# Scores of four heads on four 32-row strips, from keys and queries transposed as channel pairs

## The chip, the cores and the metric

One core of a Trainium2 chip runs the whole program. The metric is device time in microseconds of one execution. The core has TensorE (PE; its weight loads are listed as PEld), VectorE (DVE), ScalarE (ACT), GpSimd (POOL) and SyncE (SP), each with its own queue in which instructions run in order, and 16 DMA engines that serve the DMA queues. TensorE reads from SBUF and writes to PSUM, which has eight banks of 2 KB per partition.

## The reference

Attention with two fixed masks, then a bilinear feed-forward layer. For 8 batches, 8 heads, 576 positions and 64 channels:

```python
scores = scale * np.matmul(q, k.transpose(0, 1, 3, 2))
mask_local = (rel >= 0) & (rel < stride)                       # heads 0 to 3, stride 32
mask_strided = (rel >= 0) & (pos[None, :] % stride == pos[:, None] % stride)   # heads 4 to 7
attn = softmax(np.where(mask, scores, -1e9))
x = (attn @ v) laid out as 4608 tokens x 512
out = ((x @ w_a) * (x @ w_b)) @ w_out                          # w_a, w_b: 512x1536, w_out: 1536x512
```

## The kernel before

**Two interleaved streams.** The feed-forward layer runs over nine tiles of 512 tokens. Each tile has 16 slots, and slots are numbered through (tile t starts at slot 16t). The first twelve slots of a tile form one 128-wide slice f of the hidden layer each: `ab_mm` (L617) multiplies by `w_a` and `w_b` (L626), ScalarE copies the first product out of PSUM (`a_sb`, L647) and VectorE multiplies it by the second into `pf` (L650). The last four slots form the output y of the tile. In tiles 0 and 1 these are plain matmuls (L892); from tile 2 on `y_plan` (L815) forms y from fourteen groups of six products (L830, the order in `Y_ORDER`), which need `pf` and sums of it that VectorE makes in `fast_s` (L754). PSUM tiles `mm` (three banks) and `tp` (one) are shared in turn by all of these; `st` and `o` have two banks each and serve the attention.

**Attention rides on the slots.** Batch b must be ready when tile b needs its tokens, so its steps are written by hand into the slots of tile b-1: table `STEPS` for batches 1 and 2, `LATER` and `IN_Y` (L584 to L592) for batches 3 to 7. A position n means after slot n; n - 0.5 means in the middle of slot n, between the products with `w_a` and `w_b`; a position in `IN_Y` counts the groups of y. What a step issues on every engine takes its place in that engine's queue there.

A batch has eight units u: two pairs of local heads (u = 0 to 3) and two of strided heads (u = 4 to 7), each in two halves. A unit takes two steps:
- `S` (L437): `S_p` multiplies keys by queries into `st` (L392), `S_x` takes the exponential on ScalarE into `p` (L413), `S_m` masks `p` on VectorE (L431).
- `V`: `V_p` multiplies `p` by the values into `o` (L470), and VectorE divides by the sums (L478, L496). For strided units from batch 2 on, and for all units of batch 2, `step_VT` (L518) is used instead: L529 forms the transposed output in `o`, ScalarE takes Ln of the sums and Exp of its negative (L538, L539), and VectorE multiplies into `xT` (L543, L545). Local units of batches 3 to 7 go to DRAM and come back transposed (`rows_out`, `rows_in`: steps O and I).

**Keys and queries from batch 2 on.** GpSimd issues loads that cast to bf16, each of the four heads of a kind on its own 32 partitions. `step_D` (L320) transposes them on VectorE in blocks of 32x32, as 2-byte elements: two calls each for local k and q (L329), three each for strided k and q (L334). After that the two halves of a head's 64 channels lie side by side, so 24 SyncE copies per batch (L346, L350) bring them to 64 partitions, the queries into `qz`, in which the other head's half stays zero. `kT` and `qz` are double-buffered. Then one matmul of 128 rows gives both heads of a pair:

```python
nc.tensor.matmul(sv[:, i, :2 * n].rearrange("p (j n) -> p j n", j=2), lhsT=kT[:, c % 2, k0:k0 + 128],
                 rhs=qz_pair[b % 2][c // 2][:, :, c % 2, k0:k0 + n], start=True, stop=True)
```

The zeros are set by memsets early on (`zero_qz`, L114) and again for batch 3 by GpSimd (`rezero`, L355). The calls `do(slot, ...)` (L1021 to L1059) place loads, transposes and memsets; where a slot has any, GpSimd first runs a one-element copy (`pace`, L1076) that waits for the slot's result. Batch 0 scores its heads one by one, each on 64 of the 128 rows (L405, for strided heads after a first product L399).

Of the kernel before, what the change touches and what calls it, by code (L numbers as in the profile page):

```python
# [9 lines left out]
I16 = mybir.dt.int16  # L10
ALU = mybir.AluOpType
# [3 lines left out]
FIRST_D = 2  # L15
# [16 lines left out]
def kernel(  # L32
# [34 lines left out]
    def open_psum(stack, **bufs):  # L67
        for nm, n in bufs.items():
# [8 lines left out]
    qz_pair = [(const.tile([128, 2, 2, S], BF16, name=f"qz{i}l"), const.tile([128, 2, 2, RS * GP], BF16, name=f"qz{i}s"))  # L77
               for i in range(2)]
    qz_buf = [[tuple(t[:, j] for t in pair) for j in range(2)] for pair in qz_pair]
    kT_buf = [(const.tile([128, 2, PAD + S], BF16, name=f"kT{i}l"), const.tile([128, 2, RS * GP + 48], BF16, name=f"kT{i}s"))  # L80
              for i in range(2)]
    vl_buf = [const.tile([128, HL * 6, VW], BF16, name=f"vl{i}") for i in range(2)]
# [15 lines left out]
    def consts(i):  # L98
        if i == 0:
            for p in p_buf:  # L100
                nc.vector.memset(p[:, :, W:], 0.0)
            nc.vector.memset(p_buf[4][:, 1, 2 * W - PW:W], 0.0)
        nc.vector.memset(kT_buf[i][0][:, :, 0:PAD], 0.0)
        nc.vector.memset(kT_buf[i][1], 0.0)
        nc.vector.memset(vl_buf[i][:, :, D:D + 1], 1.0)
        nc.vector.memset(vs_buf[i][:, :, :, D:D + 1], 1.0)
        nc.vector.memset(vl_buf[i][:PAD, 0, 0:D], 0.0)
# [4 lines left out]
    spare = qz_buf[0][0][0][:, 0]  # L112

    def zero_qz(i, eng, parts=((0, 0), (0, 1), (1, 0), (1, 1))):  # L114
        for j, z in parts:
            t = qz_buf[i][j][z]
            if (i, j, z) == (0, 0, 0):
                t = t[:, 1]
            if eng is nc.scalar:
                nc.scalar.copy(t, spare[:, :1].unsqueeze(2).to_broadcast(list(t.shape)))  # L120
            else:
                eng.memset(t, 0.0)
# [176 lines left out]
    def T_e(b, c, nm):  # L299
        tv = held.pop((b, c, nm))  # L300
        if c < 2:
            perm = lambda t: t.rearrange("d (p r) -> d p r", r=RL)
        else:
            perm = lambda t: t.rearrange("d (g p) -> d g p", p=GP)[:, :, :NP]
        if nm == "k":
            t = kT_buf[b % 2][c // 2][:, c % 2]
            (nc.scalar.copy if b == 1 and c < 2 else nc.vector.tensor_copy)(perm(t[:, PAD:] if c < 2 else t[:, :RS * GP]), tv)
        elif b == 0:
            if c % 2 == 0:
                tl[b, c // 2, nm] = blocks("q", c // 2)  # L310
            nc.scalar.copy(perm(tl[b, c // 2, nm][:, c % 2]), tv)
        else:
            for j in range(2):
                pr = slice(64 * j, 64 * j + 64)
                nc.scalar.copy(
                    perm(qz_buf[b % 2][j][c // 2][pr, c % 2]), tv[pr])
# [3 lines left out]
    def step_D(b, z, nm, part):  # L320
        src = nats.get((b, nm, z == 1))
        if part == 0:
            tl[b, z, nm] = blocks(nm, z)
        t = tl.get((b, z, nm))
        if part is None:
            last = True
        elif z == 0:
            i = slice(NY // 2 * part, NY // 2 * (part + 1))
            nc.vector.transpose(t.rearrange("p h (i y) -> p i h y", i=NY)[:, i],  # L329
                                src[:, i].rearrange("p i (h d) -> p i h d", h=2))  # L330
            last = part == 1
        else:

            nc.vector.transpose(  # L334
                t.rearrange("p h (r c) -> p r h c", r=RS)[:, :, :, YS * part:YS * part + 32],
                src[:, part].rearrange("p (r h d) -> p r h d", r=RS, h=2))
            last = part == 2
        if last:
            for nm, c in {"k": (("k", 0),), "q": (("q", 0), ("k", 1), ("q", 1)), "r": (("k", 1), ("q", 1))}[nm]:
                if part is not None and z == 1 and c == 1 and b > FIRST_D:  # L340
                    continue
                t = tl[b, z, nm]
                for e in range(2):
                    if nm == "k":
                        dst = kT_buf[b % 2][z][64 * e:64 * e + 64, c]
                        nc.sync.dma_start(out=dst[:, PAD:] if z == 0 else dst[:, :RS * GP], in_=t[64 * c:64 * c + 64, e])  # L346
                        continue
                    for j in range(2):
                        r0 = 64 * c + 32 * j
                        nc.sync.dma_start(out=qz_buf[b % 2][j][z][64 * e + 32 * j:64 * e + 32 * j + 32, c],  # L350
                                          in_=t[r0:r0 + 32, e])
                if (nm, c, z) == ("q", 0, 0) and b - 1 > FIRST_D:
                    rows_in(b - 1, 1)

    def rezero(b):  # L355

        for j in range(2):
            for t in qz_buf[b % 2][j]:
                nc.gpsimd.memset(t[32:64] if j == 0 else t[64:96], 0.0)
# [19 lines left out]
    def p_cols(b, p, j, i, n, w):  # L379
        return p[:, j, i * n:i * n + w] if b == 0 else p_flat(p)[:, (2 * i + j) * n:(2 * i + j) * n + w]  # L380

    def S_p(b, u):
# [5 lines left out]
        if b > 0:  # L388
            sv = st.rearrange("p a (i n) -> p (a i) n", n=256)
            for i in range(G):  # L390
                k0 = (G * half + i) * (LW if c < 2 else GP)
                nc.tensor.matmul(sv[:, i, :2 * n].rearrange("p (j n) -> p j n", j=2), lhsT=kT[:, c % 2, k0:k0 + 128],  # L392
                                 rhs=qz_pair[b % 2][c // 2][:, :, c % 2, k0:k0 + n], start=True, stop=True)
            return
# [13 lines left out]
    def S_x(b, u):  # L408
# [3 lines left out]
        if b > 0:  # L412
            nc.scalar.activation(p_flat(p)[:M, :2 * W].rearrange("p (i n) -> p i n", n=2 * n),  # L413
                                 st[:M].rearrange("p a (i n) -> p (a i) n", n=256)[:, :G, :2 * n], ACT.Exp, scale=scale)
            return
        nc.scalar.activation(p[:M, :, :W], st[:M, :, :W], ACT.Exp, scale=scale)

    def S_m(b, u):
        c, half, M, n, G = unit(u)
        p = ps[b, u]  # L420
        at_j = 1 if b == 0 else 2
        shape = [M, 2, G, n] if b == 0 else [M, G, 2, n]
# [4 lines left out]
        if b == 0:  # L427
# [14 lines left out]

    def V_p(b, u):
# [11 lines left out]
        else:  # L455
            o = psum4["o"].tile([128, 2, 512], F32, tag="o", name="o")
# [61 lines left out]
    def step_VT(b, u):  # L518
# [3 lines left out]
        o = psum4["o"].tile([128, 2, 512], F32, tag="o", name="o")  # L522
# [45 lines left out]
    def step_X(b, c):  # L568
# [16 lines left out]
                 10: "V6 Tk0", 10.5: "Tq0 Pk1 Z0", 11: "Pq1", 12: "V7 Tk1 S0 W0 W1", 12.5: "Tq1 W2",  # L585
                 12.6: "S1", 12.75: "L0 X2", 13: "s2 X3 V0 m2 L1 W3", 13.5: "V1 S3", 14: "V2 X0", 14.5: "V3 D1", 15: "X1"},
             2: {20: "S0", 20.5: "S1", 21.5: "V0", 22: "S2", 23: "V1", 23.5: "S3", 24.5: "V2", 25: "S4", 26: "V3", 26.5: "S5",
                 27.5: "V4", 28: "S6", 28.5: "V5", 29: "S7", 29.5: "V6", 30.5: "V7"}}
    LATER = {-1: "S0", 0: "S1", 1: "V0", 2: "S2", 3: "V1 O0", 4: "S3 I0", 5: "V2", 6: "S4", 7: "V3 O1", 8: "S5", 9: "V4",
             10: "S6",  # L590
             11: "V5"}
    IN_Y = {2: "S7", 6: "V6", 11: "V7"}  # L592
    FN = {"Tk": step_Tk, "Tq": step_Tq, "S": step_S, "V": step_V, "X": step_X, "W": lambda b, n: fast_w(n, slice(0, 3)),
          "s": S_px, "m": S_m, "L": lead_vl, "O": rows_out, "I": rows_in, "Pk": lambda b, c: pair_up("k", c), "Pq": lambda b, c: pair_up("q", c),
          "Z": lambda b, n: zero_qz(0, nc.vector, ((1, 1),)), "D": lambda b, n: step_D(FIRST_D, 0, "k", n)}
# [33 lines left out]
    def ffn_ab(t, f, mid, ab=None):  # L629
# [21 lines left out]
        else:  # L651
# [6 lines left out]
              + [t.rearrange("p a b c -> p (a b c)")[:, :12 * 128] for t in qz_pair[0]]]  # L658
    xsum = {t: qz_pair[1][t - 7].rearrange("p a b c -> p (a b c)")[:, :8 * HT].rearrange("p (n c m) -> p n c m", n=4, c=2)
# [261 lines left out]
    with tc.manual_schedule(engines={ENG.PE, ENG.SP, ENG.Pool, ENG.DVE, ENG.Activation}):  # L921
# [20 lines left out]
        zero_qz(1, nc.scalar, ((0, 1),))  # L942
# [9 lines left out]
        for nm in ORDER:  # L952
# [24 lines left out]
            elif nm == "Z":  # L977
                zero_qz(1, nc.scalar, ((0, 0),))
# [25 lines left out]
        steps[16 * (B - 2) + 9][-1][1].append("I1")  # L1004
# [16 lines left out]
        for b in range(FIRST_D, B):  # L1021
            g0 = 16 * (b - 2)
            if b == FIRST_D:
                do(0, load_qk, b, False)
                do(1, load_qk, b, True)
                do(16, load_vl, b)
                for h in range(HL):
                    do(20 + h, load_vs, b, (h,))
            else:
# [5 lines left out]
            gs = {2: (14, 14, 15, 15, 16, 16, 17, 17, 18, 18), 3: (8, 9, 10, 11, 12, 13, 14, 15, 16, 17)}.get(b) or (  # L1035
                3, 5, 7, 9, 12, 13, 14, 15, 16, 17)
            for (z, nm, part), g in zip(((0, "k", 0), (0, "k", 1), (0, "q", 0), (0, "q", 1), (1, "k", 0), (1, "k", 1),
                                         (1, "k", 2), (1, "q", 0), (1, "q", 1), (1, "q", 2)), gs):
                if (b, z, nm, part) != (FIRST_D, 0, "k", 1):
                    do(g0 + g, step_D, b, z, nm, part)  # L1040
            if b > FIRST_D:
                do(g0 + 19, step_D, b, 1, "r", None)
# [9 lines left out]
        do(1, zero_qz, 1, nc.vector, ((1, 1),))  # L1052
        do(4, zero_qz, 1, nc.vector, ((1, 0),))
        for i, jz in ((2, (0, 0)), (3, (1, 0)), (0, (0, 1))):
            do(i, zero_qz, 0, nc.vector, (jz,))
        do(14, rezero, 1)
# [53 lines left out]
```

## Time and profile before

| | |
|---|---|
| time, median of 3 runs | 326.2 us (325.67 to 326.99) |
| span of the profiled execution, first to last instruction | 324.3 us |
| runs' median less that span | 1.9 us |
| granted TensorE clock | 0.999 |
| busy: DVE, ACT, POOL | 259.9, 190.9, 162.7 us |
| moved by DMA | 40.44 MB; mean 125 GB/s |
| L413, exp of a unit | 56 times, 650 ns |
| L431, mask of a unit | 32 times 454 ns, 28 times 448 ns |
| L329 and L334, transposes | 24 times 766 ns; 36 times about 703 ns |

The profile comes from one execution, whose own time is known as its span; the runs beside it were not profiled. A line of a timeline gives start, length, engine, line of the code, operation, what is written and read, shapes, and how many instructions were merged into it. A TensorE row's length is the time from start to result, 190 to 380 ns for one matmul, while the next one starts long before that: how fast matmuls follow each other is seen only from their starts. Some records of matmuls are missing.

### The profile page before, as it was taken

The numbers are of one execution on the slowest core, as the hardware profiler recorded it, in microseconds if no ns is written. First come the engines' busy times: TensorE is split into PE (matmuls) and PEld (weight loads), VectorE is DVE, ScalarE is ACT, GpSimd is POOL, SyncE is SP. The second block draws the span as 40 slices with busy tenths as digits, with TensorE's granted clock in tenths as the row PEclk, the third lists the DMA queues.
The fourth block names the chain that finished last, engine by engine and source line by source line (L and its number), as shares of the span: only waits on it lengthen the run. The fifth ranks groups of instructions, "written<-read, shape, count | busy, mean of one in ns | idle before, by whom it ended". The sixth has DMA issues, their size and how long they took to land.

```text
span 324.3 us, 7477 instructions
## 1 busy us (share of the span) xinstructions
PE 316.7 (98%) x2669; PEld 211.2 (65%) x2698; DVE 259.9 (80%) x563; ACT 190.9 (59%) x338; POOL 162.7 (50%) x293
## 2 busy tenths in 40 slices
PE   8999999999999999999999999999999999999994
PEld 7764555455555577556999895559555866786684
DVE  6766797888878988898889888988999667857862
ACT  6762776468674576447654765467546655535541
POOL 8844938689948534762576338734004003202520
PEclk9999999999999999999999999999999999999999
DMA  8999999899999999999899999999137030004004
GB/s 154 138 203 195 203 191 173 169 173 143 133 224 124 147 88 99 107 187 179 94 111 183 183 108 92 158 205 131 30 81 166 20 115 18 0 2 129 1 3 129
DMA packets 110725, 40.44 MB, mean 125 GB/s; under 512 B 88672, under 2 KB 107744, under 8 KB 110688
## 3 DMA queue, kind: packets, MB, share of 16 engines
q0 software_dynamic: 85968, 19.48, 66.0%
q1 hardware_dynamic: 24576, 20.42, 24.9%
q8 instruction: 21, 0.34, 0.4%
q14 instruction: 16, 0.13, 0.1%
q10 hardware_dynamic: 144, 0.07, 0.1%
HBM read 39.51 MB, written 10.91 MB: 155 GB/s over the span
## 4 chain that ended last, share of the span: by engine, by line
PE 88%; DMA 5%; POOL 4%; DVE 1%; issue 1%; ACT 1%; POOLq 0%
PE mm L626 42%; PE mm L830 17%; PE mm L892 6%; PE mm L710 5%; DMA wb_sb<-in_moe_w_b_dram 5%; PE st L392 4%; PE ax L703 3%; PE mm L703 2%; PE o L529 2%; PE o L470 2%; PE mm L857 2%; POOL shared L197 1%; PE end L857 1%; POOL wa_sb L252 1%; POOL vl L225 1%
## 5 line engine op out<-in xcount | busy, mean ns | idle before, releaser
L626 PE MATMUL mm<-xT,wb_sb 128*128 128x512 bf16 (+1 forms) x381 | 88.2, 352 | 0.7 <-DMA wb_sb<-in_moe_w_b_dram 0.4
L626 PE MATMUL mm<-xT,wa_sb 128*128 128x512 bf16 (+1 forms) x367 | 86.6, 351 | 0.8
L647 ACT COPY a_sb<-mm 128x512 f32<-128x512 f32 x84 | 49.2, 586 | 47.6 <-PE mm L626 45.6
L626 PEld LDWEIGHTS <-wb_sb 128*128 128x128 bf16 x392 | 37.8, 98 | 34.3 <-DMA wb_sb<-in_moe_w_b_dram 1.1
L1076 POOL CAST pace<-pf 1x1 f32<-1x1 bf16 x82 | 24.5, 298 | 64.3 <-DVE pf L650 42.7
L626 PEld LDWEIGHTS <-wa_sb 128*128 128x128 bf16 x392 | 35.1, 98 | 21.1
L650 DVE TENSOR_TENSOR pf<-a_sb,mm 128x512 bf16<-128x512 f32 x62 | 42.1, 679 | 7.3 <-PE mm L626 6.1
L413 ACT ACTIVATE p<-st 72x576 bf16<-72x576 f32 (+1 forms) x56 | 36.4, 650 | 14.4 <-PE st L392 14.2
L545 DVE TENSOR_TENSOR xT<-o,xr 64x288 bf16<-64x288 f32 x48 | 21.4, 446 | 14.8 <-ACT xr L539 14.5
L830 PEld LDWEIGHTS <-ps 128*128 128x128 bf16 x288 | 28.0, 98 | 3.1
L795 ACT COPY y_sb<-mm 128x512 f32<-128x512 f32 (+1 forms) x28 | 15.6, 556 | 17.6 <-PE mm L830 15.0
L830 PE MATMUL mm<-wf,ps 128*128 128x256 bf16 x216 | 25.5, 273 | 0.0
L710 PE MATMUL mm<-xT,wb_sb 128*128 128x512 bf16 x83 | 25.3, 379 | 0.1
L538 ACT ACTIVATE xr<-o 64x576 f32<-64x576 f32 x28 | 18.1, 648 | 12.1 <-PE o L529 11.9
L892 PE MATMUL mm<-wo_sb,pf 128*128 128x512 bf16 x93 | 23.1, 379 | 0.2
L243 POOL DMA_DIRECT2D vs<-in_v_dram x24 | 19.7, 820 | 4.8 <-PE mm L830 2.4
L830 PEld LDWEIGHTS <-pf 128*128 128x128 bf16 x216 | 20.3, 98 | 2.5 <-issue 0.2
L1076 POOL COPY pace<-y_sb 1x1 f32<-1x1 f32 x23 | 4.6, 200 | 33.1 <-DVE y_sb L793 20.1
L539 ACT ACTIVATE xr<-xr 64x576 f32<-64x576 f32 x28 | 19.1, 683 | 0.9
L652 DVE TENSOR_TENSOR pf<-a_sb,mm 128x512 bf16<-128x512 f32 x22 | 14.9, 677 | 4.8 <-ACT a_sb L647 2.7
L212 POOL DMA_DIRECT2D kl<-in_k_dram x24 | 16.0, 667 | 5.2 <-issue 2.9
L830 PE MATMUL mm<-wo_sb,pf 128*128 128x256 bf16 x144 | 18.5, 273 | 0.1
(189 smaller groups left out, 598.0 us busy)
## 6 DMA issues: line engine op xcount, KB each, us to landing
out_dram<-y_sb SPq DMA_DIRECT2D x12, 512.0 KB, 4.8
out_dram<-y_sb SPq DMA_DIRECT2D x11, 256.0 KB, 3.9
vl<-in_v_dram POOLq DMA_DIRECT2D x6, 384.0 KB, 7.8
kl<-in_k_dram POOLq DMA_DIRECT2D x24, 72.0 KB, 3.1
ql<-in_q_dram POOLq DMA_DIRECT2D x24, 72.0 KB, 3.2
vs<-in_v_dram POOLq DMA_DIRECT2D x24, 72.0 KB, 4.3
wo_sb<-in_moe_w_out_dram POOLq DMA_DIRECT2D x4, 384.0 KB, 9.5
natk<-in_k_dram POOLq DMA_DIRECT2D x20, 72.0 KB, 3.6
```

The source lines that it names most:

```text
L243: nc.gpsimd.dma_start(out=vs_buf[b % 2][:, h, :, 0:D], in_=v[b, HL + h].rearrange("(p r) d -> p r d", r=RS))
L413: nc.scalar.activation(p_flat(p)[:M, :2 * W].rearrange("p (i n) -> p i n", n=2 * n), st[:M].rearrange("p a (i n) -> p (a i) n", n=256)[:, ...
L538: nc.scalar.activation(r, sums, ACT.Ln)
L539: nc.scalar.activation(r, r, ACT.Exp, scale=-1.0)
L545: nc.vector.tensor_mul(dst.rearrange("d (p r) -> d p r", r=RS)[:, :, G * half:G * (half + 1)], o[:64, j, :W].rearrange("d (g p) -> d p g", ...
L626: nc.tensor.matmul(ps_[:, c0:c0 + n], lhsT=w[:, kk, 128 * f:128 * (f + 1)], rhs=xT[:, kk, x0:x0 + n], start=(kk == first and c0 == 0), sto ...
L647: nc.scalar.copy(a_sb, ab[0])
L650: nc.vector.tensor_mul(pf[:, f, :].rearrange("p (i a s) -> p a i s", i=2, s=16), halves(a_sb), halves(ab[1]))
L710: nc.tensor.matmul(got[e], lhsT=wb_sb[:, kk, 128 * f:128 * (f + 1)], rhs=xT[:, kk, x0:x0 + TTOK], start=kk == 0, stop=kk == KD - 1)
L830: nc.tensor.matmul(bank[b][:, q], lhsT=lhs(g, q), rhs=rhs(g), start=k in "172" and q == 0 and g == 0, stop=g == FG - 1, skip_group_check=True)
L892: nc.tensor.matmul(ybank[j], lhsT=pf[:, f, 128 * j:128 * (j + 1)], rhs=wo_sb[:, f], start=(f == 0), stop=(f == FD - 1))
L1076: nc.gpsimd.tensor_copy(pace, done)
```

## The change

From batch 2 on:
- `step_D` transposes 4-byte elements, that is pairs of neighbouring channels: one call for local k, one for local q, one for strided q and three for strided k. A head's 32 channel pairs then lie on its own 32 partitions, with even and odd channels alternating along the row, and stay there. The 24 copies, `rezero`, one of the two `qz` pairs and its memsets go.
- A new step, `step_S4`, makes the scores of all four heads of a kind and one half at once: two units, one in `st` and one in `o`. For each block i, first with the even and then with the odd channels, four matmuls run on rows 0, 32, 64 and 96, each head into its own bank, and the odd ones are added to the even ones. Then come two exps and two masks, which use the layout of `p` that batch 0 has (one bank of 288 columns per head). The steps A0, A1 (local) and B0, B1 (strided) stand for them.
- Since `st` and `o` are now filled together, `o_tile` lets a V step write to `st` for the first pair of heads and to `o` for the second; the V steps come in pairs half a slot apart. All positions are set anew.
- Buffers: the even batches' transposed k and q get new tiles, the odd ones use the remaining `qz` pair and the strided `kT` of buffer 0. Later reuses of those tiles by the feed-forward layer are moved accordingly.

```diff
+    def step_D(b, z, nm, part=None):
+        lq, sq, sk = (t.rearrange("p t e -> p (t e)").bitcast(I32) for t in kq_buf[b % 2])
+        src = nats[b, nm, z == 1]
+        if z == 0:
+            nc.vector.transpose(lq[:, S:] if nm == "k" else lq[:, :S], src.rearrange("p i d -> p (i d)").bitcast(I32))
+        elif nm == "q":
+            nc.vector.transpose(sq, src.rearrange("p t n -> p (t n)").bitcast(I32))
+        else:
+            for i in range(3) if part is None else (part,):
+                nc.vector.transpose(sk[:, :RS * GP].rearrange("p (r c) -> p r c", r=RS)[:, :, YS * i:YS * i + 32],
+                                    src[:, i].bitcast(I32).rearrange("p (r d) -> p r d", r=RS))
...
+    def step_S4(b, z, half):
+        n, w, G = ((LW, LW, 3), (NP, GP, 4))[z]
+        sts = [pst.tile([128, 2, 512], F32, tag="st", name="st"), psum4["o"].tile([128, 2, 512], F32, tag="o", name="st")]
+        lq, sq, sk = kq_buf[b % 2]
+        for i in range(G * half, G * half + G):
+            k0 = S - PAD + LW * i if z == 0 else GP * i
+            for e in range(2):
+                for h in range(HL):
+                    r = slice(32 * h, 32 * h + 32)
+                    if z == 0:
+                        lhs, rhs = lq[r], lq[r, LW * i:LW * i + LW, e]
+                    else:
+                        lhs, rhs = sk[r], sq[r, :, e].rearrange("d (p r c) -> d r p c", r=RS, c=32)[:, i, :, :YS]
+                    nc.tensor.matmul(sts[h // 2][:, h % 2, (i % G) * n:(i % G + 1) * n], lhsT=lhs[:, k0:k0 + 128, e], rhs=rhs, start=e == 0, stop=e == 1)
+        for c in range(2):
+            u = 4 * z + 2 * c + half
+            held[b, "st", u] = sts[c]
+            S_x(b, u)
+        for c in range(2):
+            S_m(b, 4 * z + 2 * c + half)
...
+    def o_tile(b, c):
+        pool, nm = ((pst, "st"), (psum4["o"], "o"))[b == 1 or c % 2]
+        return pool.tile([128, 2, 512], F32, tag=nm, name="o")
...
-             2: {20: "S0", 20.5: "S1", 21.5: "V0", 22: "S2", 23: "V1", 23.5: "S3", 24.5: "V2", 25: "S4", 26: "V3", 26.5: "S5",
-                 27.5: "V4", 28: "S6", 28.5: "V5", 29: "S7", 29.5: "V6", 30.5: "V7"}}
-    LATER = {-1: "S0", 0: "S1", 1: "V0", 2: "S2", 3: "V1 O0", 4: "S3 I0", 5: "V2", 6: "S4", 7: "V3 O1", 8: "S5", 9: "V4",
-             10: "S6",
-             11: "V5"}
-    IN_Y = {2: "S7", 6: "V6", 11: "V7"}
+             2: {18: "A0", 19.5: "V0", 20: "V2", 21.5: "A1", 23: "V1", 23.5: "V3", 25: "B0", 26.5: "V4", 27: "V6", 28.5: "B1",
+                 30: "V5", 30.5: "V7"}}
+    LATER = {-1: "A0", 0.5: "V0", 1: "V2", 3: "A1", 4.5: "V1 O0", 5: "V3 O1", 7: "B0 I0", 8: "I1", 8.5: "V4", 9: "V6"}
+    IN_Y = {1: "B1", 5: "V5", 7: "V7"}
...
-                do(16, load_vl, b)
+                do(15, load_vl, b)
                 for h in range(HL):
-                    do(20 + h, load_vs, b, (h,))
+                    do(18 + h, load_vs, b, (h,))
...
-            gs = {2: (14, 14, 15, 15, 16, 16, 17, 17, 18, 18), 3: (8, 9, 10, 11, 12, 13, 14, 15, 16, 17)}.get(b) or (
-                3, 5, 7, 9, 12, 13, 14, 15, 16, 17)
+            gs = {2: (14, 15, 17, 18), 3: (9, 11, 13, 16)}.get(b) or (5, 8, 12, 15)
...
-        do(14, rezero, 1)
```

## The prediction

> **What bounds the kernel now.** I read the page's busy rows, then the chain that ended last, then the timeline of the windows that the change touches.
>
> ```profile
> PE 316.7 (98%) x2669; PEld 211.2 (65%) x2698; DVE 259.9 (80%) x563; ACT 190.9 (59%) x338; POOL 162.7 (50%) x293
> ...
> PE 88%; DMA 5%; POOL 4%; DVE 1%; issue 1%; ACT 1%; POOLq 0%
> ```
>
> TensorE is busy 98% of 324.3 us and is 88% of the chain, at a granted clock of 0.999. Between 30 and 290 us its timeline shows one wait worth naming (0.3 us, at 184.66, below); the other holes, of 0.22 us, are single missing records. So only two things count: how long TensorE streams, and whether it now waits. Work taken from VectorE, SyncE, GpSimd and the DMA queues buys nothing by itself.
>
> **Score stream, what goes.** Timeline of TensorE, two old score steps (columns: start, length, engine, line, shapes, count):
>
> ```profile
> 66.36 0.41 PE L392 MATMUL st<-qz0l,kT0l 128*128 128x192 bf16 x3
> ```
> ```profile
> 208.23 0.41 PE L392 MATMUL st<-qz0s,kT0s 128*128 128x144 bf16 x4
> ```
>
> A merged row's length is the starts plus one duration (246 and 226 ns). So a local matmul costs (0.41-0.246)/2 = 0.082 us and a strided one (0.41-0.226)/3 = 0.061. A batch has 12 and 16: 0.98 + 0.98 = 1.96 us.
>
> **What comes.** 112 matmuls of 32 rows: 12 groups of four at 96 columns, 16 at 72. No row has 32-row strips; the nearest are batch 0's scores (L399, L405), pairs on two 64-row halves:
>
> ```profile
> 10.43 0.46 PE L155 MATMUL misc<-const-bfloat16-1.0 128*128 128x224 bf16 x3
> 10.82 0.30 PE L405 MATMUL st<-tq,kT0l 64*128 64x96 bf16 x6
> ...
> 12.07 0.29 PE L405 MATMUL st<-tq,kT0s 64*128 64x72 bf16 x8
> 12.29 0.43 PE L296 MATMUL tp<-ident,shared 72*128 72x72 bf16 x8
> ```
>
> Six matmuls in 0.30 us are three pairs (0.30-0.21)/2 = 0.045 apart, later ones 0.040; eight in 0.29 are four pairs (0.29-0.19)/3 = 0.033 apart. Both halves run at once. But entering and leaving costs: the last L155 starts at 10.63 (two steps of 0.10), L405 only 0.19 later; the last pair at 12.07 starts at 12.17, and L296 0.12 later where its own step is 0.03. That is 0.095 us per crossing, the same at every change between full rows and halves in that stage. The new steps are entered and left 4 times a batch: 8 x 0.095 = 0.76 us.
> - If four strips run as two did: 12 x 0.043 + 16 x 0.033 = 1.04, plus 0.76 = 1.80: 0.16 us less per batch, **-1.0 us** over six batches.
> - Upper end, two pairs one after the other: 2.08 + 0.76 = 2.84: +5.3 us. It also stands for a penalty of reading every second element, which no moving operand of this trace does (stationary ones do, at L830, without loss).
> - Lower end, no crossing cost between strips and full rows: -5.5 us.
>
> I take the first: the rows show two halves starting 3 to 4 ns apart and no sign of a second limit.
>
> The Trainium skill speaks against that ("TensorE: Matmul & The Clock Gate", Measured speedup vs the span model): four row tiles gave 3.07 times, not 4. By it, as an estimate, a group would take 1.3 times as long, 0.31 us more per batch and 1.9 us more in all; the 64-row pairs here show no such loss, and no run here has four.
>
> **VectorE, queues, at nothing.** Per batch 4 transposes of 0.766 and 6 of 0.703 us (7.28 us) become two of 576 elements, one of 768, three of 256. The two old sizes differ by 63 ns for 64 elements, so about 1 ns each and 0.2 fixed: 3.85 us if a 4-byte element costs the same, 6.5 if double. Either is less. SyncE loses 24 copies a batch (3 to 4.7 us to landing each), GpSimd four memsets of 1.1 us. TensorE waited for none of them, so: zero. One transfer loses cover: batch 2's vl load, 6.6 us to landing. Without the memsets it issues near 58.5 (61.3 before) and lands near 65.1; V0, pulled to the middle of slot 20 (64.6 + 0.45 + 0.86), needs it at 65.9. It is worth 0.8 us of slack.
>
> **The waits that come.** A new score step fills `st` and `o` together, so both half-results before it must have left, and V steps come in pairs half a slot apart. One V step's chain, tile 5:
>
> ```profile
> 214.09 0.42 PE L529 MATMUL o<-p,vs 72*128 72x72 bf16 x8
> ...
> 214.55 0.65 ACT L538 ACTIVATE xr<-o 64x576 f32<-64x576 f32 x1 [0.54 <-PE o L529]
> ...
> 215.23 0.68 ACT L539 ACTIVATE xr<-xr 64x576 f32<-64x576 f32 x1
> 215.94 0.59 ACT L647 COPY a_sb<-mm 128x512 f32<-128x512 f32 x1
> 215.95 0.91 DVE L545 TENSOR_TENSOR xT<-o,xr 64x288 bf16<-64x288 f32 x2 [0.90 <-ACT xr L539]
> ...
> 217.90 0.68 DVE L650 TENSOR_TENSOR pf<-a_sb,mm 128x512 bf16<-128x512 f32 x1
> 218.06 0.42 PE L529 MATMUL o<-p,vs 72*128 72x72 bf16 x8
> ```
>
> From the V matmuls: Ln at +0.46, Exp to +1.82, VectorE's products to +2.77, then `o` is free. Call the first V of a pair 0, in the middle of a slot. The second starts at 0.25 + 0.87 = 1.12. ScalarE's order is Ln, Exp (to 1.82), a_sb (to 2.44), then Ln, Exp of the second, to 3.83; its products end at 4.78.
> - Batch 2: V0, V2, then A1 1.5 slots after V2, wanted at 1.12 + 0.25 + 1.73 + 0.87 = 3.97, possible at 4.8: 0.85 us. V1, V3, B0: a_sb is out of the way, o is free at 4.1: 0.2. V7 in the middle of slot 31, batch 3's A0 at its end: V7 comes 1.55 after V5, its Exp ends at 3.5, products at 4.4; A0 is wanted at 3.1: 1.4. Before, S0 there needed `st` alone. Sum 2.45. Behind each waits all of TensorE's queue, which is in order.
> - Batches 3 to 7, V4 in the middle of slot 9, V6 at its end: a_sb(10) ends at 4.45, V6's products at 4.78, a fast_s (0.41) at 5.2, pf(10) (0.68) at 5.87. The y part begins at 1.12 + 0.25 + 2 x 1.73 = 4.84 and its sixth product, at 5.39, needs pf(10): 0.55 us. Before, V4 stood 4.2 us ahead of y and pf(10) came 0.2 early (218.58). In tile 4 the first product already waits, for pf(10)'s bank, as it did before (y would have followed V5's eighth matmul at 184.38):
>
> ```profile
> 183.93 0.68 DVE L650 TENSOR_TENSOR pf<-a_sb,mm 128x512 bf16<-128x512 f32 x1
> ...
> 184.12 0.43 PE L529 MATMUL o<-p,vs 72*128 72x72 bf16 x8
> ...
> 184.66 0.38 PE L830 MATMUL mm<-wo_sb,pf 128*128 128x256 bf16 x2
> ```
>
> There it is 1.1. So 4 x 0.55 + 1.1, less the 0.3 that was there: 3.0.
> - In y, B1's two exps (1.3 us) now stand ahead of the copy that frees X for product 6: it ends 0.2 after it is wanted, five times: 1.0.
>
> **Sum.** -1.0 + 2.45 + 3.0 + 1.0 = +5.4 us on the span of 324.3: 329.7. The runs' median is 1.9 longer than this span, so 326.2 + 5.4 = **331.6 us**.
>
> **Rivals.**
> - Not slower: the distances suffice. From 1.0 us of waiting in all the balance turns. VectorE is freer by 3.4 us a batch; if pf(10) is not held behind the second V's products and the batch 2 steps find `o` free, only the stream is left: -1.0 - 0.3, 324.9; with free crossings too, 320.4. For it: old pairs left PE no wait but one. Against: ScalarE's two chains of 1.35 and a copy are in order, whatever VectorE does.
> - Four strips are limited to two at a time (or by strided reads): 331.6 + 6.3 = 337.9. Against: pairs 3 ns apart.
> - The crossing is cheap for strips, the waits stand: 331.6 - 4.5 = 327.1.
> - Half of the waits: 328.4.
>
> **Chances.** Forecast (329 to 335) 0.48; half of the waits 0.11; cheap crossing 0.06; slow strips 0.10; not slower 0.25. Within 0.5% (1.6 us, about what a measurement of this kernel can tell from no change) lie most of the cheap crossing (0.05) and 0.09 of the not-slower case: same 0.14; its other 0.16 is faster; slower 0.70. The range runs from 323.5, where about 0.08 of the not-slower case lies below, to 336, short of the slow strips: some 0.18 is left out.
>
> **What will show it.** Score rows (L372): 24 matmuls merged in about 0.46 us if strips run at once, 0.7 if in pairs; an L372 step that starts 0.31 us after the last 512-column start, where 0.22 is the plain step, shows a crossing. Waits: the old 0.3 us before the first L830 grows and appears before each y's sixth product; ScalarE's Ln, Exp, a_sb, Ln, Exp without a hole; a hole of 1.4 us before the score step at the end of tile 1. TensorE's busy share falls while VectorE's drops below 80%. I am wrong if L372's groups are far from 0.04 us, or if TensorE still runs without holes.

## The result and the profile after

The changed kernel takes **330.65 us** (median of 4 runs, 330.36 to 331.09); the kernel before took 326.4 us beside it. The ratio is 1.0145, with an interval of [1.012, 1.017]. In a later series on one chip it was 331.03 against 325.38 us, 1.0188 [1.0156, 1.0221]. The forecast was 331.6 us. The profiled spans are 329.4 and 324.3 us, 5.1 us apart.

The first and the fourth part of the page after, the busy row and the chain that ended last:

```profile
PE 317.4 (96%) x3173; PEld 205.2 (62%) x3202; DVE 242.8 (74%) x536; ACT 187.2 (57%) x338; POOL 153.0 (46%) x285
...
PE 73%; DMA 8%; POOL 6%; ACT 6%; DVE 3%; issue 2%; POOLq 0%; ACTq 0%
```

VectorE lost 17 us of work and went from 80% to 74%, DMA moved 33.0 MB and not 40.4, and the time did not gain by it. TensorE's busy time hardly changed (316.7 to 317.4 us); the span grew around it. In the chain TensorE fell from 88% to 73%, and ScalarE and VectorE now hold 9% of it: TensorE waits for them. The view of TensorE's waits (who waits, for whom, us in total, times, longest) names them:

```profile
PE mm L830 <- DVE pf L650: 2.0, 5, 0.8
PE st L372 <- DVE xT L547: 1.0, 1, 1.0
...
PE st L372 <- DVE xT L545: 0.5, 1, 0.5
```

These idle times are counted from the modelled end of the matmul ahead. Below, a **hole** is what a start is late by against the plain step (0.216 us after 512 columns, 0.109 after 256, 0.004 between the strips of one group), which is what the span pays: 2.94 us in all before L830, 1.25 and 0.75 before L372.

**The score steps.** Timeline of TensorE in the changed kernel, a local step and a strided one, each with the full-row matmuls around it:

```profile
231.05 1.47 PE L830 MATMUL mm<-wo_sb,ps 128*128 128x256 bf16 x12
232.45 0.44 PE L372 MATMUL st<-qz1l 32*128 32x96 bf16 x24
232.83 0.39 PE L626 MATMUL mm<-xT,wa_sb 128*128 128x512 bf16 x1
```
```profile
222.92 0.45 PE L372 MATMUL st<-kq 32*128 32x72 bf16 x32
223.30 0.50 PE L830 MATMUL mm<-wo_sb,pf 128*128 128x256 bf16 x3
```

Twenty-four matmuls fill 0.44 us up to the last result, thirty-two 0.45: four strips do run at once. In the single records the four matmuls of a group mostly start 2 to 6 ns apart and the groups some 0.0437 us apart (96 columns) and 0.033 (72); only the first group of a step takes longer, 0.056 and 0.040. From a step's first start to the next full-row start it is 0.371 and 0.380 us (median of the steps that nothing held), and the first start itself comes 0.095 us later than a full-row matmul would. The first full-row matmul behind the strips takes 0.226 us to the next start and not 0.216, which no old step shows. That makes 2 x 0.371 + 2 x 0.380 + 4 x 0.095 + 4 x 0.010 = 1.92 us a batch. The eight old steps, counted in the same way from the first start to the next full-row start, took 4 x 0.248 + 4 x 0.250 = 1.99, so the stream gains some 0.4 us over six batches.

**The V chain before y**, tile 5, the place shown of before:

```profile
216.83 0.42 PE L531 MATMUL o<-p,vs 72*128 72x72 bf16 x8
...
217.29 0.65 ACT L540 ACTIVATE xr<-o 64x576 f32<-64x576 f32 x1 [1.31 <-PE o L531]
...
217.97 0.68 ACT L541 ACTIVATE xr<-xr 64x576 f32<-64x576 f32 x1
...
218.67 0.58 ACT L647 COPY a_sb<-mm 128x512 f32<-128x512 f32 x1
...
219.28 0.65 ACT L540 ACTIVATE xr<-o 64x576 f32<-64x576 f32 x1
...
219.96 0.68 ACT L541 ACTIVATE xr<-xr 64x576 f32<-64x576 f32 x1
220.67 1.07 ACT L647 COPY a_sb<-mm 128x512 f32<-128x512 f32 x2
220.68 0.91 DVE L547 TENSOR_TENSOR xT<-o,xr 64x288 bf16<-64x288 f32 x2 [0.36 <-ACT xr L541]
...
221.67 0.71 PE L830 MATMUL mm<-wo_sb,pf 128*128 128x256 bf16 x5
221.97 0.68 DVE L650 TENSOR_TENSOR pf<-a_sb,mm 128x512 bf16<-128x512 f32 x1
...
222.71 0.28 PE L830 MATMUL mm<-wo_sb,pf 128*128 128x256 bf16 x1 [0.33 <-DVE pf L650]
```

ScalarE runs Ln, Exp, a_sb, Ln, Exp, a_sb without a hole from 217.29 on. VectorE ends V6's products at 221.6, y begins at 221.67, and pf(10) starts only at 221.97, behind a sum for y. So y's sixth product, due at 222.21, starts at 222.71. Before, pf(10) was 0.2 us early here.

### The profile page after: what moved, and what is told of

Same layout as the page of the kernel before. It is cut to its first block, busy times and chain, and to the rows that moved or that the text cites. A ratio compares the mean times of both kernels' runs of the same rounds, so it can differ in the third digit from the quotient of the medians.

```text
span 329.4 us, 8142 instructions
## 1 busy us (share of the span) xinstructions
PE 317.4 (96%) x3173; PEld 205.2 (62%) x3202; DVE 242.8 (74%) x536; ACT 187.2 (57%) x338; POOL 153.0 (46%) x285
## 4 chain that ended last, share of the span: by engine, by line
PE 73%; DMA 8%; POOL 6%; ACT 6%; DVE 3%; issue 2%; POOLq 0%; ACTq 0%
PE mm L626 33%; PE mm L830 16%; PE mm L710 5%; DMA wb_sb<-in_moe_w_b_dram 4%; DMA vl<-in_v_dram 4%; PE mm L892 4%; PE ax L703 3%; PE st L372 3%; ACT xr L540 2%; ACT xr L541 2%; PE mm L703 2%; POOL shared L202 2%; PE o L531 2%; PE mm L857 2%; PE o L472 1%
## 5 line engine op out<-in xcount | busy, mean ns | idle before, releaser
L647 ACT COPY a_sb<-mm 128x512 f32<-128x512 f32 x84 | 48.6, 585 | 45.1 <-PE mm L626 44.7
L626 PEld LDWEIGHTS <-wb_sb 128*128 128x128 bf16 x392 | 36.8, 98 | 31.1 <-issue 0.2
L1068 POOL CAST pace<-pf 1x1 f32<-1x1 bf16 x80 | 18.0, 225 | 73.3 <-DVE pf L650 56.2
L414 ACT ACTIVATE p<-st 128x576 bf16<-128x576 f32 (+1 forms) x56 | 33.7, 646 | 21.3 <-PE st L372 19.1
L830 PEld LDWEIGHTS <-ps 128*128 128x128 bf16 x288 | 27.9, 98 | 3.2
L830 PE MATMUL mm<-wf,ps 128*128 128x256 bf16 x216 | 26.4, 273 | 0.0
L830 PEld LDWEIGHTS <-pf 128*128 128x128 bf16 x216 | 20.4, 98 | 7.0 <-DVE pf L650 2.3
L1068 POOL COPY pace<-y_sb 1x1 f32<-1x1 f32 x21 | 5.6, 268 | 37.2 <-DVE y_sb L793 19.0
L892 PE MATMUL mm<-wo_sb,pf 128*128 128x512 bf16 x93 | 22.4, 379 | 0.3 <-issue 0.2
L830 PE MATMUL mm<-wo_sb,pf 128*128 128x256 bf16 x144 | 19.2, 273 | 2.0 <-DVE pf L650 2.0
L429 DVE TENSOR_TENSOR p<-p,mask_l 128x576 int16<-128x576 int16 x32 | 14.6, 455 | 8.8 <-ACT p L414 7.1
```

Source lines behind the costliest of these rows:

```text
L626: nc.tensor.matmul(ps_[:, c0:c0 + n], lhsT=w[:, kk, 128 * f:128 * (f + 1)], rhs=xT[:, kk, x0:x0 + n], start=(kk == first and c0 == 0), sto ...
L647: nc.scalar.copy(a_sb, ab[0])
L830: nc.tensor.matmul(bank[b][:, q], lhsT=lhs(g, q), rhs=rhs(g), start=k in "172" and q == 0 and g == 0, stop=g == FG - 1, skip_group_check=True)
L892: nc.tensor.matmul(ybank[j], lhsT=pf[:, f, 128 * j:128 * (j + 1)], rhs=wo_sb[:, f], start=(f == 0), stop=(f == FD - 1))
L1068: nc.gpsimd.tensor_copy(pace, done)
```

## Experiments

All times are medians beside runs of the kernel before on the same chip (325.4 to 325.8 us there); the ratio to it and its interval follow. The changed kernel itself stands at 1.0145 in one series and at 1.0188 in the other, so a difference of one run from it is known to about 0.4%, and the traces say where it lies.

### The spacing of batch 2

```diff
-             2: {18: "A0", 19.5: "V0", 20: "V2", 21.5: "A1",
+             2: {17.5: "A0", 19: "V0", 19.5: "V2", 21.5: "A1",
...
+    LATER3 = {0: "A0", 1: "V0", 1.5: "V2", 3: "A1", 4.5: "V1 O0", 5: "V3 O1", 7: "B0 I0", 8: "I1", 8.5: "V4", 9: "V6"}
...
-            for pos, names in (STEPS.get(b) or {16 * (b - 1) + x: n for x, n in LATER.items()}).items():
+            for pos, names in (STEPS.get(b) or {16 * (b - 1) + x: n for x, n in (LATER3 if b == 3 else LATER).items()}).items():
...
-                do(15, load_vl, b)
+                do(14, load_vl, b)
```

> Of the changed kernel (330.65 us) only the spacing in batch 2 and at the start of batch 3 is edited: A0, V0, V2 of batch 2 half a slot earlier (its vl load one slot earlier, so that V0 finds its data), so that A1 comes 2 slots after V2 and not 1.5; batch 3's A0 at the end of slot 32 and not 31, its V0 and V2 half a slot later. My theory (the loss is TensorE waiting for ScalarE and VectorE to empty st and o): the 0.71 us hole before A1 at 71.2 and the 1.21 us hole before the score step at 95.3 go, 330.65 - 1.9 = 328.7 us. Rival (the loss is in the stream of the strips, and the holes only show where the queue stands): the waits reappear at the moved steps, 330.6 us.

Measured: **328.69 us**, 1.0098 [1.0081, 1.0115]. The two steps in the changed kernel, whose third matmul, the first one into `o`, is held:

```profile
70.42 0.22 PE L372 MATMUL st<-kq 32*128 32x96 bf16 x2
...
71.17 0.43 PE L372 MATMUL st<-kq 32*128 32x96 bf16 x22 [0.54 <-DVE xT L545]
```
```profile
94.05 0.22 PE L372 MATMUL st<-qz1l 32*128 32x96 bf16 x2
95.31 0.43 PE L372 MATMUL st<-qz1l 32*128 32x96 bf16 x22 [1.04 <-DVE xT L547]
```

And in this run:

```profile
70.03 0.44 PE L372 MATMUL st<-kq 32*128 32x96 bf16 x24
```
```profile
94.69 0.44 PE L372 MATMUL st<-qz1l 32*128 32x96 bf16 x24
```

Both holes are gone and nothing took their place. The loss there is the wait for `o`, as the theory had it. The held matmul is the third of its group and due 0.004 us after the second, so the holes are 0.75 and 1.25 us, together 2.0; the text above counts 0.71 and 1.21 by the step between groups. The gain, 0.5 to 0.9% (1.5 to 2.9 us) against the two measurements of the changed kernel, fits that.

### The pair before y, moved as a whole

```diff
-    LATER = {-1: "A0", 0.5: "V0", 1: "V2", 3: "A1", 4.5: "V1 O0", 5: "V3 O1", 7: "B0 I0", 8: "I1", 8.5: "V4", 9: "V6"}
+    LATER = {-1: "A0", 0.5: "V0", 1: "V2", 3: "A1", 4.5: "V1 O0", 5: "V3 O1", 6.5: "B0 I0", 7.5: "I1", 8: "V4", 8.5: "V6"}
```

> Of the changed kernel only B0, V4 and V6 of batches 3 to 7 are moved, half a slot earlier each (the end of slot 7 to its middle, the middle of 9 to the end of 8, the end of 9 to its middle). My theory: the a_sb copy of slot 10 then no longer stands between the two ScalarE chains, pf(10) is ready ahead of the sixth product of each y part, and the waits there (0.48, 0.50, 0.98, 0.49, 0.49 us, of which 0.27 was in the kernel before) go: 330.65 - 2.6 = 328.0 us. Rival (pf(10) is late because of the sums that VectorE makes for y, or the wait is one for the X bank): the waits stay, 330.6 us.

Measured: **330.4 us**, 1.0147 [1.0133, 1.0161]: nothing gained. The cure failed, and the cause was still open. At the sixth product of tile 5 the hole shrank from 0.49 to 0.15 us, but TensorE's timeline in tile 2 of this run has a new one, before y:

```profile
116.69 1.03 PE L626 MATMUL mm<-xT,wa_sb 128*128 128x512 bf16 x4
118.17 1.02 PE L626 MATMUL mm<-xT,wb_sb 128*128 128x512 bf16 x4 [0.46 <-DVE pf L650]
```

Slot 11's second half is 0.62 us late, for the bank that pf(9) frees. The holes of the five tiles are 0.62, 0.62, 0.63, 0.15 and 0.90, together 2.92 us; they were 2.94. The delay travels with the pair and comes out at the next place where something waits for pf.

### Both edits

The first two edits together, in `LATER3` too.

> Both spacings at once. My theory: the two gains add, 330.65 - 1.9 - 2.6 = 326.2 us, the time of the kernel before (326.4), since what is left of the change is the score stream, which by the trace is worth about 0.5 us. Rival (the strips themselves cost the 4 us): 330.6 us. If only the waits of batch 2 or only those of y were real holes, 328.0 to 328.7.

Measured: **328.42 us**, 1.0093 [1.0078, 1.0108], the first edit's gain and no more. The holes of batch 2 and 3 are gone, those of the tiles are as in the second run. At batch 2's V0, half a slot earlier here, a hole of 0.42 us appeared: its vl load, issued one slot earlier, took 8.8 us to landing. In the first run it stands at the same places, took 7.6 and made no hole. There is little slack on that side.

### The pair taken apart

With the edit of batch 2 kept:

```diff
-    LATER = {-1: "A0", 0.5: "V0", 1: "V2", 3: "A1", 4.5: "V1 O0", 5: "V3 O1", 7: "B0 I0", 8: "I1", 8.5: "V4", 9: "V6"}
+    LATER = {-1: "A0", 0.5: "V0", 1: "V2", 2.5: "A1", 4: "V1 O0", 4.5: "V3 O1", 6: "B0", 7: "V4 I0", 8: "I1", 9: "V6"}
+    LATER3 = {0: "A0", 1: "V0", 1.5: "V2", 3: "A1", 4.5: "V1 O0", 5: "V3 O1", 6.5: "B0", 7: "I0", 7.5: "V4", 8: "I1", 9: "V6"}
```

> The spacing of batch 2 and of batch 3's A0 as in the run that set them apart (worth 1.5 to 1.9 us), and for batches 4 to 7 V4 at the end of slot 7 and V6 at the end of slot 9 (2 slots apart and not 0.5; B0 at the end of slot 6, A1, V1, V3 half a slot earlier); batch 3: V4 in the middle of slot 8, V6 as it was. Moving the pair as a whole by half a slot only moved the wait (the sixth product of y waited 0.15 in the place of 0.49, but slot 11's second half waited 0.62 for the bank that pf(9) frees). My theory, now: it is the pair that does it, two chains of Ln and Exp (1.33 us each) and an a_sb copy of 0.6 in one slot of 1.73 us, so that pf falls 1.5 us behind wherever the pair stands; apart, both the wait at y and the one at slot 11 go: 0.5 to 1.0 us shorter in each of five tiles, about 2.6 us less than with the spacing of batch 2 alone, 326.0 us where the kernel before takes 325.5. Rival (pf is late for VectorE's own load, its sums for y): the waits stay in some place, 328.4 to 328.7.

Measured: **326.48 us**, 1.0024 [1.0007, 1.0041]. Tile 5 of this run (one line number on):

```profile
217.05 0.68 DVE L651 TENSOR_TENSOR pf<-a_sb,mm 128x512 bf16<-128x512 f32 x1
217.62 0.82 PE L831 MATMUL mm<-wo_sb,pf 128*128 128x256 bf16 x6
```

pf(10) starts at 217.05, before y and not 0.3 us into it, and the first six products run through. Of the 2.94 us two holes of 0.16 and 0.12 us are left. V6 stands at the same position as in the changed kernel, and V4 moved away from it. In batches 4 to 7 A1, V1, V3 and B0 moved too. Batch 3 settles it. There A1, V1 and V3 stand where they stood, A0, V0 and V2 moved as in the first run, where this hole stayed at 0.49 us, and B0 is half a slot earlier as in the run that moved the pair as a whole, which gained nothing. New is V4, one slot earlier and 1.5 slots ahead of V6, and the hole of tile 2 is gone. So it is the pair, two chains of 1.33 us and a copy of 0.6 in a slot of 1.73, that made the waits before y, not V6's place and not VectorE's sums for y, which are all still there.

### VectorE's relief

Around all transposes of `step_D`:

```diff
+        for _ in range(2):
```

> The changed kernel with each of VectorE's 4-byte transposes of batches 2 to 7 issued twice (the second writes the same data again): 3.84 us more of VectorE per batch, 23 us in all, about 0.4 us per batch more than the old transposes took. My theory (VectorE's relief is worth nothing, another work hides it): 330.6 us, within 0.5. Rival (the relief is what keeps the loss at 4 us, since VectorE's products and pf stand behind those transposes): more than 1.5 us longer, 332 to 336 us.

Measured: **331.44 us**, 1.0183 [1.0169, 1.0197], where the changed kernel itself has 1.0188 in its series:

> The changed kernel itself, beside the others on the same chip: 1.0145 times the kernel before. By my theory the waits at the same steps return to within 0.1 us; what differs from profile to profile (the 0.77 us at batch 1's V steps, where the vl load lands) is no part of the change.

(331.03 us; the holes at the same steps within 0.01 us, at batch 1's V0 0.36 and not 0.77.) VectorE's busy time goes from 243 to 263 us, above that of the kernel before, and of these 20 us little reaches the time: by the two measurements of the changed kernel 0 to 0.4%. The trace of the doubled run shows where. In tiles 2 to 6 the holes before y are the same to 0.01 us. In tile 1, where batch 2's transposes stand close together, two holes cost 0.9 us more:

```profile
65.54 1.98 DVE L332 STREAM_TRANSPOSE kq<-natq 128x768 int32<-128x768 int32 x2
...
67.45 0.65 DVE L653 TENSOR_TENSOR pf<-a_sb,mm 128x512 bf16<-128x512 f32 x1
...
68.15 1.02 PE L627 MATMUL mm<-xT,wb_sb 128*128 128x512 bf16 x4 [0.45 <-DVE pf L653]
```

The second copy of a transpose of 0.97 us holds back a pf, and TensorE is 0.61 us late for it; the hole before A1 grows from 0.75 to 1.01. So VectorE's relief is worth nothing from batch 3 on and at most this 0.9 us in batch 2; the rival's 1.5 us and more did not come.

### What a crossing costs

```diff
         for i in range(G * half, G * half + G):
+            if i == G * half + 2:
+                nc.tensor.matmul(sts[0][:, 0, 400:464], lhsT=ident, rhs=ident[:, :64], start=True, stop=True)
```

The control has `if i == G * half` in its place. The added product is part of no result.

> In every score step of four strips a full-row matmul of 64 columns (written to unused columns of the same bank) stands behind the second group of four or eight, so that TensorE leaves the strips and enters them once more per step: 24 more exits and 24 more entries. My theory (a crossing costs about 0.095 us each way): 24 x 0.19 = 4.5 us more than the run with the same matmul ahead of the step. Rival (the 0.095 us is a start of the step, as a wait for the bank, and not the change of rows): the same time as that run.

> The same full-row matmul of 64 columns ahead of every score step of four strips, next to full-row matmuls, so that no crossing is added: the control of the run that splits the strips. 64 columns at the rate of the 96 and 72 column groups (0.043 and 0.033 us) are some 0.03 us, 24 times: 0.7 us more than the changed kernel, at most 1.5. If it costs as much as the split, the price is that of any added matmul.

Measured: **336.4 us**, 1.0338 [1.0319, 1.0357], with the matmul in the middle, **331.49 us**, 1.0185 [1.0166, 1.0204], with it in front, 0.5 us more than the changed kernel on that chip. The difference between the two is 4.9 us, 0.205 per step. A local step of the split run:

```profile
236.97 0.35 PE L374 MATMUL st<-qz1l 32*128 32x96 bf16 x16
237.25 0.20 PE L365 MATMUL st<-ident 128*128 128x64 bf16 x1
237.39 0.27 PE L374 MATMUL st<-qz1l 32*128 32x96 bf16 x8
```

Four groups, the first of 0.056 and three of 0.0437, are 0.187 us, yet the full-row matmul starts 0.283 after the first: leaving the strips took 0.095. Its 64 columns are some 0.03, yet the strips go on 0.136 later: 0.105. In the control they go on 0.125 after it, which is the same 0.03 and 0.095, so a full-row matmul behind strips takes 0.010 longer itself. The step lasts 0.62 us, in the control 0.37. The 0.095 us of the changed kernel is the price of the change of rows, each way, and no other start of the step. With the 0.010 and the 0.013 of a longer first group one visit costs 0.21 us, and the measured 0.205 agrees. The Trainium skill ("TensorEngine Tiling (Array Packing)", Key Properties) says that a change of tiling mode drains TensorE; the runs agree.

### Do the strips really run side by side

In `step_S4`, head, then block, then even or odd:

```diff
-        for i in range(G * half, G * half + G):
-            k0 = S - PAD + LW * i if z == 0 else GP * i
-            for e in range(2):
-                for h in range(HL):
+        for h in range(HL):
+            for i in range(G * half, G * half + G):
+                k0 = S - PAD + LW * i if z == 0 else GP * i
+                for e in range(2):
```

> The score step of four strips with its loops turned: head by head, so that all matmuls of one strip of 32 rows come one after the other and two strips never stand side by side in the queue; the same 24 or 32 matmuls, the same crossings. By the trace of the changed kernel a group of four strips starts every 0.043 us (96 columns) and its members 3 to 6 ns apart. My theory (four strips really run at once, that is what the stream gains): a step takes 24 x 0.043 = 1.03 us and not 0.27, some 0.75 us more in each of 24 steps, +18 us, 349 us. Rival (the rate is set by something other than the strips, such as the loads of the weights at 0.09 us for four): within 3 us of the changed kernel.

Measured: **339.68 us**, 1.0433 [1.0418, 1.0448]: 8.7 us more than the changed kernel's 331.03, half of what was expected, and far above the rival's 3. A step now lasts 0.687 (local) and 0.835 us (strided), 0.32 and 0.455 longer, 12 x 0.32 + 12 x 0.455 = 9.3 us, less 0.4 by which the two holes before L372 shrank; the profiled spans are 8.6 and 9.5 us apart from the two of the changed kernel. Here is the local one:

```profile
104.32 0.75 PE L372 MATMUL st<-qz1l 32*128 32x96 bf16 x24
105.01 1.04 PE L626 MATMUL mm<-xT,wa_sb 128*128 128x512 bf16 x4
```

So the gain of running together is real, but one strip after the other is not 1.03 us. In the single records of a local step the starts are about 0.043 us apart at the beginning and the end, where one strip is at work, and 0.02 in the middle. A strided step shows more: at both ends no two starts are closer than 0.031 us, but the sixth start comes 0.009 after the fifth, so another strip is at work from there on, while the first still has matmuls to do. A record does not tell its strip. But the sixth is also the first whose record is some 13 ns longer than most, as that of the step's very first matmul is, and the next such records are the 14th and the 22nd, each time three places ahead of the written 9th, 17th and 25th. Read so, the next strip's first matmul overtakes the last three of the strip ahead, and two strips run side by side even when the program has them one behind the other. Then TensorE's matmuls do not all run in the order of its queue, as the start of this document has it: those of different strips can pass each other.

### Batch 1's vl load

The changed kernel has two holes that the prediction did not have, at batch 1's V0, slot 13 (0.41 and 0.36 us):

```profile
51.04 0.19 PE L472 MATMUL o<-vl,p 128*128 128x65 bf16 x1 [0.24 <-DMA vl<-in_v_dram]
51.43 0.31 PE L472 MATMUL o<-vl,p 128*128 128x65 bf16 x5 [0.19 <-DVE vl L236]
```

The load takes 13.9 us to landing there, 12.4 in the kernel before, though the change touches neither it nor its neighbours. First try, on the kernel with the pair apart (the last lines let GpSimd wait for slots 11 and 12 too before it issues a load):

```diff
-                do(0, load_qk, b, False)
-                do(1, load_qk, b, True)
+                do(11, load_qk, b, False)
+                do(12, load_qk, b, True)
-            if i > 13 and i in at and done is not None:
+            if i > 10 and i in at and done is not None:
```

> The kernel with V4 and V6 set apart (326.5 us), and batch 2's loads of k and q for the local channels issued behind slots 11 and 12 instead of 0 and 1, so that batch 1's vl load, which lands 13 to 14 us after its issue, has the queue with wo_sb alone. My theory (the two holes at batch 1's V0, 0.34 + 0.35 us, are that load arriving late with its neighbours on the same 16 engines): both go, 325.8 us; the kernel before takes 325.4. Rival (the load is late for wo_sb, ahead of it in the queue): 326.5 us. If the delayed loads come too late for slot 14's transposes, longer by what TensorE then waits.

Measured: **327.02 us**, 1.0043 [1.0029, 1.0057]. The k loads now issue at 45.1 and not 38.5 us, the load still takes 13.8, the holes stay (0.60 and 0.36). That theory fell.

> The kernel before, for a second profile of it: in the first its vl load of batch 1 took 12.4 us to landing and TensorE did not wait at batch 1's V0, where the changed kernel's profiles have 13.1 to 13.9 us and holes of 0.35 to 0.77 us. If those holes belong to the change, this profile has none; if they come and go with the transfers, it may have them too.

12.5 us, and no hole (span 323.3 us). Then the places in memory:

```diff
+    const.tile([128, 160], BF16, name="pad")
...
-    spare = const.tile([128, 2], BF16, name="spare")
+    spare = const.tile([128, 256], BF16, name="spare")
```

> The kernel with V4 and V6 set apart (326.5 us), and nothing changed in its instructions: 320 bytes of padding behind the new kq tiles, and spare made 512 bytes, so that every tile behind them starts at the same offset within 512 bytes per partition as in the kernel before (vl1 at 0; in the changed kernel at 192, the weights at 160 where they had 448). The kernel before waited for batch 1's vl load in neither of its two profiles (12.4 and 12.5 us to landing), the kernels of the change did in seven of ten, with 13.1 to 13.9 us to landing wherever it was read; holding the neighbouring loads back did not help. Theory now (the load is slower because the rows of 128 bytes that it writes, and the weights' of 768 and 1,024, start elsewhere): landing 12.5 us, the two holes of 0.34 and 0.35 us go, 325.8 us; the kernel before takes 325.4 to 325.6. Rival (the places don't matter; head and loads merely shift against each other): 13.1 to 13.9 us to landing, 326.5 us.

(Over all profiles of the change it is seven of eleven that had the holes.) Measured: **326.06 us**, 1.0009 [0.9988, 1.003]. The DMA view of the stretch in which the load issues (KB, us to landing), of the changed kernel, of the pair apart, and of the pair apart with the padding:

```profile
vl<-in_v_dram POOLq DMA_DIRECT2D x1, 288.0 KB, 13.9
```
```profile
vl<-in_v_dram POOLq DMA_DIRECT2D x1, 288.0 KB, 13.4
```
```profile
vl<-in_v_dram POOLq DMA_DIRECT2D x1, 288.0 KB, 12.2
```

The load lands in 12.2 us, and V0 runs without a hole; TensorE reached V0 13.0 us after the load's issue in this run and 13.1 in the one without padding, so it is the load that came sooner. In the ten profiles with the shifted tiles where its landing could be read it took 13.1 to 13.9 us, in the three with the old offsets 12.2 to 12.5. The 0.7 us of holes are gone; the time itself is 0.4 us less, which the intervals don't tell apart, and the profiled spans are 324.8 with the padding and 324.7 without. There is one profile with the padding, so the link of landing and offsets rests on these thirteen profiles together. Whether vl's own offset counts or that of the weights ahead of it in the queue was not separated.

## Why the prediction was right

The time was 1 us below the forecast (the forecast was +5.4 us; the spans are 5.1 apart), and the reasons held in the main. By its steps:

- **TensorE and its waits alone count; relief of the others is worth zero.** Right but for batch 2: TensorE's share fell, VectorE's too, as named, and the doubled transposes cost nothing from batch 3 on, 0.9 us in tile 1. Their own length was right: 0.766, 0.971 and 0.445 us for the three sizes, 3.84 us a batch where 3.85 was worked out.
- **Score stream, -1.0 us.** Mis-sized: -0.4. Four strips run as two halves did and the crossing costs 0.095 us, as taken. The new steps take 1.92 us a batch and not 1.80: each of the four visits has a first group 0.013 longer and a first full-row matmul behind it 0.010 longer, and some 0.005 go into the stagger of four matmuls in the last group. Neither slow strips nor a cheap crossing, the rivals, came true. Within a series of groups four strips are four times as fast as one: groups of 96 columns start 0.0437 us apart, and one strip alone, at the ends of the turned loops, 0.043. By the Trainium skill's 3.07 times ("TensorE: Matmul & The Clock Gate", Measured speedup vs the span model) the groups would start, as an estimate, some 0.056 us apart; at 96 columns the trace does not agree.
- **Batch 2 and the start of batch 3, +2.45 us.** 2.00: A1 0.75 (0.85 forecast), batch 3's A0 1.25 (1.4), B0 nothing (0.2). Shown by spacing them.
- **pf(10) before y, +3.0 us.** 2.67: 0.48, 0.50, 0.98, 0.49 and 0.49 us, less the 0.27 that was there before. Shown by taking the pair apart, after moving it had not helped.
- **The copy behind B1's exps, +1.0 us.** Failed: no such wait. The two exps took 1.18 us and not 1.3, and in tile 5 the copy ends at 225.06 us, 0.2 before product 6 is due (223.97 + 12 x 0.108 = 225.27), and not 0.2 after.
- **Batch 2's vl load, 0.8 us of slack.** It held: the load took 6.6 us, and there is no hole at V0 in the changed kernel.
- **Not foreseen:** batch 1's vl load, 0.77 us in the first profile and 0.36 in the second; the thirteen profiles tie it to where the new tiles push the old ones.

In the profile the terms give -0.4 + 2.00 + 2.67 + 0.77 = 5.0 of the 5.1 us. Two smaller shifts outside them nearly cancel: TensorE came to batch 1's V0 0.35 us sooner than in the first profile of the kernel before, and what follows 296 us (there 292) took 0.5 longer. That the sum came so close is luck in part: 1.8 us of waiting that did not come (0.45 in batch 2, 0.35 before y, 1.0 behind B1) stood against 0.6 of stream and 0.8 of a late load. The mechanism, TensorE waiting for the chains behind pairs of V steps, is not luck: the spacing runs take it away. With nearly all waits gone the kernel takes about as long as the one before (326.06 against 325.78 us): the 0.4 us of stream that the trace shows are less than the runs can tell. In the three profiles with the pair apart TensorE starts its last matmul at 319.2 to 319.4 us, in the two of the kernel before at 319.7 and 318.7; but from there to the end of the program it is 5.5 to 5.8 us and not 4.6, which no run here explains.

## What to carry to other kernels

Four strips of 32 rows ran at full speed here, but each entry and each exit cost 0.1 us: count the visits as well as the matmuls, and let the four strips of a group follow each other in the program. Where a step needs two buffers at once, look at the distance of the steps that empty them: a pair in one slot made the next step wait at both places that were tried, and with 1.5 to 2 slots between them 0.3 of the 2.9 us were left. And after a change of buffers, look at how long untouched loads take.

## What the runs showed of the hardware

- A visit to the 32-row strips between full-row matmuls costs 0.21 us beside its groups: 24 more visits took 4.9 us.
- TensorE started matmuls of another strip ahead of earlier ones of a busy strip: by the starts and the lengths of the records, the sixth start and not the ninth.
- The load of vl, in rows of 128 bytes, took 13.1 to 13.9 us to landing in ten profiles and 12.2 to 12.5 in three, as the tiles' offsets within 512 bytes went.
- Every second 2-byte element as moving operand costs next to nothing: the groups start 0.0437 us apart for 96 columns and 0.033 for 72, where batch 0's halves, with neighbouring elements, have 0.042 and 0.032.
